# One attention kernel, three double score tiles: two of them take scores and pairs of row maxima by turns

## The chip, the core and the metric

The kernel runs on one core of one Trainium2 chip. It is one launch that computes a whole transformer block in float32 (most matmuls read fp32r operands that were split into a high and a low part, so that three products stand for one exact one). The metric is device time in microseconds. Before the change it is 1136.1 us, the median of three runs between 1134.84 and 1137.12. Five engines work side by side, each in the order of its own queue: TensorE (PE; PEld is its weight load), VectorE (DVE), ScalarE (ACT), GpSimd (POOL) and SyncE (SP), which issues nearly all DMAs. PSUM, into which TensorE writes, has 8 banks of 128 x 512 float32; all of this case turns on who holds which bank for how long.

## The reference, cut to what matters

One sequence of S = 2048 tokens, D = 448, H = 16 heads of 28, a hidden width F = 1792:

```python
h = layernorm(x) * (1 + ca) + sa                 # sa, ca, ga, sb, cb, gb from silu(c) @ w_mod
q, k, v = split(h @ wqkv)                        # 16 heads of 28
p = softmax(q @ k^T * 28 ** -0.5)                # 16 x 2048 x 2048
x = x + ga * ((p @ v) @ wo)
h = layernorm(x) * (1 + cb) + sb
x = x + gb * (gelu(layernorm(h) @ w1 + b1) @ w2 + b2)
```

The softmax needs the maximum of every row of scores before the exponential of that row is taken. The kernel finds these maxima in a pass of its own, from the high parts of q and k alone, and then computes the scores a second time, exactly, with the negated maximum as one more row of the product.

## The kernel before, in words

The program has three stages. In the first one (about 175 us) q, k and v are computed and the first maxima are taken. The second one is the attention: 16 units, each of one group g of four heads and one quarter qt of 512 queries, and in each unit 16 steps of 128 keys, 256 steps in all. The third one is the MLP.

A step of the attention (lines 1142 to 1183 of the kernel before) does this, and the order in which the lines stand is the order of each engine's queue, since the schedule is written out by hand.

- Scores of 128 keys by 512 queries for four heads: each head has a row group of the PE array (32 of its 128 rows). Two halves of two heads (`hf`, rows 0 to 63 and 64 to 127) go each into one double tile of two banks (`ps_s2`, lines 90 to 93), three products per head (`term`): 12 matmuls at line 1163. ScalarE takes the exponential of a whole double tile in one instruction (line 1168) and writes half of the tile of probabilities `pt`.
- Row maxima, three or four of them (`n_maxima`, line 1122): each is a matmul of one head's 128 queries by 512 keys into one single bank (`max_mm`, line 466) and a VectorE reduction of 128 x 512 to one column (`max_one`, line 471). `emit_max` (line 565) takes them from the queue `mxq`; those beside the first half are from heads of the other half, those behind the second half are from heads of the first.
- The product of the probabilities of the step before with v (`av`, line 1133): 4 matmuls in the program, 8 in the trace (float32 takes two), into the bank `o`. The text calls it AV.
- What the schedule `sched` has for the step (line 1182): the end of a unit (division by the row sums, DMAs through DRAM), the projection with `wo` in four steps of each of the last four units (`t_wo`, line 912: 9 or 12 matmuls at line 386 into a single bank, a copy by ScalarE at line 926), preparation of weights.

The maxima of the next unit have to be complete six steps before it begins: `finish_max` (line 610, called at line 1147) takes what is still missing, one after the other.

The 8 banks in this stage before: `o` has one, the maxima have three single banks by turns (`mx_ring`: m1, m2, m2), the scores have two double tiles (`s_ring`: s1, s0). Once all maxima are taken, `third_tile` (line 800) gives the two banks of m2 to a third double tile s2 for the scores. `slot` gives buffers in SBUF by name: `pt` goes round d0, c0 and c1, which hold other things in the first and the third stage.

## Time and profile before

| what | us |
|---|---|
| median of three runs | 1136.1 |
| span of the profiled execution | 1133.1 |
| runs, lowest to highest | 1134.84 to 1137.12 |
| attention, the 232 stretches from AV to AV that have maxima in them (175.15 to 770.95) | 595.8 |
| TensorE busy over the span | 1123.2 |
| VectorE busy over the span | 843.6 |
| ScalarE busy over the span | 671.4 |

The profile is of one execution, whose span is 3.0 us below the median of the runs. Its parts are: busy time by engine; the chain of work that ended last; groups of instructions by line, with their number, busy time, mean duration in ns and the idle time before them; the waits (who waited for whom: total us, times, longest); windows (busy us of PE, PEld, DVE, ACT, POOL in a stretch, with counts, the granted clock as a share of full speed, and the DMA share); and the timeline (start in us, duration in us, engine, line, operation, names, number of instructions merged into the row). A row of the timeline that merges several instructions has the start of the first and the time until the end of the last. Matmuls are pipelined, so TensorE shows as busy nearly all the time even where it waits; where a matmul starts says more than how busy the engine is.

### The profile page before, as it was taken

How to read it: one execution, taken by the hardware profiler on the slowest of the kernel's cores; microseconds unless marked ns; L12 is line 12 of the kernel's file. 1: busy time of each engine (PE TensorE's matmuls, PEld its weight loads, DVE VectorE, ACT ScalarE, POOL GpSimd, SP SyncE). 2: the span in 40 equal slices, each digit the busy share in tenths (PEclk: the TensorE clock that was granted, in tenths of full speed). 3: DMA queues.
4: the chain of work that ended last, by engine and by line, in shares of the span. 5: the costliest groups of instructions: out<-in, count | busy, mean ns of one | idle time of the engine just before them, and what ended most of it. 6: DMA issues, size and time to landing. Idle time of an engine off the chain costs nothing.

```text
span 1133.1 us, 20660 instructions
## 1 busy us (share of the span) xinstructions
PE 1123.2 (99%) x8319; PEld 673.8 (59%) x8319; DVE 843.6 (74%) x1485; ACT 671.4 (59%) x823; POOL 209.8 (19%) x211
## 2 busy tenths in 40 slices
PE   9999999999999999999999999999999999999998
PEld 6756674444444444444444454545468888888887
DVE  6868788999999999999999978595348853444322
ACT  4555667777777877787787867576862321211110
POOL 2533332010000000000000010207114503123000
PEclk9999999999999999999999999999999999999999
DMA  8562263121221211211111312020422100000000
GB/s 309 203 206 77 86 213 100 46 85 39 68 84 57 58 39 57 86 57 58 48 48 57 104 49 76 11 85 1 136 57 86 43 33 1 1 33 1 33 1 33
DMA packets 49341, 81.19 MB, mean 72 GB/s; under 512 B 12311, under 2 KB 18702, under 8 KB 49234
## 3 DMA queue, kind: packets, MB, share of 16 engines
q1 hardware_dynamic: 48762, 79.14, 22.2%
q8 instruction: 65, 1.06, 0.4%
q10 hardware_dynamic: 148, 0.46, 0.1%
q0 software_dynamic: 336, 0.28, 0.1%
q14 instruction: 30, 0.25, 0.1%
HBM read 55.04 MB, written 26.48 MB: 72 GB/s over the span
## 4 chain that ended last, share of the span: by engine, by line
PE 93%; DVE 3%; DMA 1%; ACT 1%; issue 1%; SPq 0%; DVEq 0%; POOL 0%; POOLq 0%; ACTq 0%
PE s L1163 27%; PE o L1133 22%; PE m L386 16%; PE pa L386 8%; PE m L466 6%; PE s L1233 3%; PE s L1232 3%; PE s L1234 3%; DVE mxp L471 2%; PE t L1233 1%; PE t L1234 1%; PE t L1232 1%; PE o L267 1%; PE ma L466 1%; DMA slot_c<-in_w_mod_dram 1%
## 5 line engine op out<-in xcount | busy, mean ns | idle before, releaser
L471 DVE TENSOR_REDUCE mxp<-m 128x1 f32<-128x512 f32 x884 | 568.8, 685 | 81.4 <-PE m L466 44.6
L1163 PE MATMUL s<-slot_b,slot_a 28*128 28x512 f32 (+1 forms) x3072 | 383.3, 422 | 0.3
L1168 ACT ACTIVATE slot_c<-s 128x1024 f32<-128x1024 f32 x340 | 329.6, 1022 | 82.4 <-PE s L1163 82.2
L1163 PEld LDWEIGHTS s<-slot_b,slot_a 28*128 28x128 f32 (+1 forms) x3072 | 216.4, 184 | 251.3 <-ACT slot_c L1168 149.4
L466 PE MATMUL m<-kh,qh 28*128 28x512 f32 x863 | 286.0, 472 | 0.9 <-DVE mxp L471 0.5
L1168 ACT ACTIVATE slot_d<-s 128x1024 f32<-128x1024 f32 x172 | 166.8, 1022 | 42.1 <-PE s L1163 42.0
L1133 PE MATMUL o<-slot_c,v 128*32 128x512 f32 x1360 | 181.2, 605 | 0.0
L1209 ACT ACTIVATE full<-m,b_col 128x512 f32<-128x512 f32 x56 | 38.6, 688 | 191.9 <-PE m L386 179.7
L1212 DVE CAST hi<-full 128x512 fp32r<-128x512 f32 x56 | 25.2, 450 | 135.2 <-ACT full L1209 135.2
L466 PEld LDWEIGHTS m<-kh,qh 28*128 28x128 f32 x863 | 114.3, 182 | 6.6 <-DVE mxp L471 4.7
L895 POOL TENSOR_TENSOR osb<-osb,osb 128x512 f32<-128x512 f32 x16 | 20.9, 1308 | 448.3 <-DMA osb<-drec 306.9
L1133 PE MATMUL o<-slot_d,v 128*32 128x512 f32 x688 | 92.5, 605 | 0.6 <-ACT osb L1102 0.4
L386 PE MATMUL m<-y,slot_a 128*128 128x512 f32 x160 | 60.7, 395 | 0.0
L1133 PEld LDWEIGHTS o<-slot_c,v 128*32 128x32 f32 x1360 | 26.8, 108 | 53.5 <-issue 52.8
L1213 DVE TENSOR_TENSOR lo<-full,hi 128x512 fp32r<-128x512 f32 x56 | 44.1, 788 | 5.9 <-DVE hi L1212 0.9
L386 PE MATMUL m<-y,slot_c 128*128 128x512 f32 x152 | 47.5, 396 | 0.1
L471 DVE TENSOR_REDUCE mxp<-ma 128x1 f32<-128x512 f32 x54 | 35.6, 682 | 7.2 <-PE m L466 4.1
L386 PE MATMUL m<-y,slot_v 128*128 128x512 f32 x112 | 39.2, 396 | 0.0
L386 PE MATMUL m<-y,slot_b 128*128 128x512 f32 x112 | 39.0, 397 | 0.0
L479 ACT ACTIVATE slot_d<-m 128x512 f32<-128x512 f32 x33 | 18.8, 597 | 31.5 <-PE m L466 18.0
L1234 PE MATMUL s<-slot_v,lo 128*128 128x448 f32 x96 | 35.0, 365 | 0.0
L1232 PE MATMUL s<-slot_v,hi 128*128 128x448 f32 x96 | 35.0, 364 | 0.0
(272 smaller groups left out, 1434.0 us busy)
## 6 DMA issues: line engine op xcount, KB each, us to landing
slot_b<-d SPq DMA_DIRECT2D x32, 256.0 KB
slot_a<-d SPq DMA_DIRECT2D x32, 256.0 KB
d<-lo SPq DMA_DIRECT2D x28, 256.0 KB
d<-hi SPq DMA_DIRECT2D x16, 256.0 KB
osb<-drec SPq DMA_DIRECT2D x15, 256.0 KB
out_dram<-xn SPq DMA_DIRECT2D x16, 224.0 KB
raw<-in_B_w_dram SPq DMA_DIRECT2D x14, 224.0 KB
qh<-d SPq DMA_DIRECT2D x12, 256.0 KB
```

The source lines that it names most:

```text
L386: pe.matmul(p, a, b, start=(i == 0), stop=(i == len(terms) - 1))
L466: pe.matmul(m, qh_sb[(g, qt)][js, i * 128 : (i + 1) * 128], k[js, :], start=True, stop=True)
L471: dve.tensor_reduce(out=mxp[(g, qt)][:, i, j, cch : cch + 1], in_=m, op=ALU.max, axis=AX.X)
L1133: pe.matmul(o[32 * j : 32 * j + 32, :], v_sb[kt // 4][:, kt % 4, 4 * g + j, :], p[:, j, :], start=(kt == 0), stop=(kt == NKT - 1),)
L1163: pe.matmul(s2[:, jj, :], ks[rows_, kp, kc], qs[rows_, qp, :], start=(term == 0), stop=(term == 2))
L1168: act.activation(pt[:, 2 * hf : 2 * hf + 2, :], s2, AF.Exp, scale=SCALE)
L1209: act.activation(gf, p, AF.Gelu_apprx_tanh, bias=b1_col[:, i : i + 1])
L1212: dve.tensor_copy(ghi, gf)
L1213: dve.tensor_tensor(out=glo, in0=gf, in1=f(ghi), op=ALU.subtract)
L1232: pe.matmul(pp, ghi[:, ts], w_hi, start=(m == 0), stop=False)
L1233: pe.matmul(pp, ghi[:, ts], w_lo, start=False, stop=False)
L1234: pe.matmul(pp, glo[:, ts], w_hi, start=False, stop=(m == NFT - 1))
```

## The change

The 8 banks of the attention stage are dealt out anew. `o` and m1 keep one bank each; s0, s1 and s2 are three double tiles from the start.

- The first half of a step's scores always goes to s0. The second half goes to s1 or s2 by turns (`now`), and the other one of these two takes a pair of maxima: two matmuls of two heads of one half, and one VectorE reduction of 128 x 2 x 512 to two columns (`emit_pair`). Single maxima have the one bank m1 (`emit_single`).
- Which half of the heads comes first changes from step to step, so that the pair behind the second half is of heads of the first one, and the single one beside the first half of heads of the second one.
- A plain step has one single maximum and one pair. In some steps (`extra`) a second single stands between the pair and AV; there the first single stands behind the third product of the first half, and in the step after such a one behind the first product of the second half.
- A step with a `wo` projection issues first a pair of maxima into s0, then a single one into one bank of the tile `now`, and the projection into its other bank: three maxima more than a plain step.
- The probabilities of a step are two tiles of half the size; those of the first half have three buffers, those of the second two. The names c0, c1 and d0 in SBUF are halved for that, also where the first and third stage use them.

The order of the built program, engine by engine, shows what comes of it in the 232 stretches from AV to AV that have maxima in them. Before: 223 plain ones, 114 with three maxima and 109 with four in turn, and nine with a projection (three or four maxima, the last one two). After: 66 plain ones with a second single, most of them every third step, 155 with three maxima, two in which `finish_max` adds 6 and 4 maxima, one after the other through m1, and nine with a projection, mostly with six maxima, two of which have 6 and 4 more from `finish_max`. The reductions of VectorE fall from 946 to 706, 240 of them pairs. No DMA is added or removed in the attention.

```diff
-    halved = ("a2", "a3", "b1")
+    halved = ("a2", "a3", "b1", "c0", "c1", "d0")
...
+    def ps_two(key):
+        return ps_pools[key][1].tile([128, 2, 512], F32, tag=key, name=nm(key), bufs=1)
...
-    def emit_max(n, half=None):
+    def emit_max(n):
...
+    def ready_max():
+        return [m for m in mxq[:24] if (m[0], m[2]) in kh_sb and m[:2] in qh_sb]
...
+    def emit_single(half, ps):
...
+        near = ready_max()
...
+        fits = [x for x, m in enumerate(near) if m[4] // 2 == half]
+        alone = [x for x in fits if whole[by_set(near[x])] == 1]
+        m = near[alone[0] if alone else fits[-2] if len(fits) > 1 else 0]
...
+        max_one(g, qt, cch, i, j, ps)
+        count(g, qt, [cch])
+
+    def emit_pair(half, t):
+        near = ready_max()
+        for a, m in enumerate(near):
+            n = m[:4] + (m[4] + 1,)
+            if m[4] == 2 * half and n in near:
...
+                for jj in range(2):
+                    max_mm(g, qt, i, j + jj, kh_sb[(g, cch)], lambda: t[:, jj])
+                dve.tensor_reduce(out=mxp[(g, qt)][:, i, j : j + 2, cch], in_=t, op=ALU.max, axis=AX.X)
+                count(g, qt, [cch, cch])
+                return
+        for jj in range(2):
+            emit_single(half, lambda: t[:, jj])
...
-    for key in ("ma", "pa"):
+    for key in ("ma", "pa", "m2"):
         ps_close(key)
     for key in ("s0", "s1"):
         ps_open(key)
-    s_ring[:] = ["s1", "s0"]
-    mx_ring[:] = ["m1", "m2", "m2"]
...
+    ps_open("s2", "right")
+    mx_ring[:] = ["m1"]
+    turns = ("s1", "s2")
...
         def t_wo(t):
             def go():
-                p = ps_mx()
+                if three:
+                    p = ps_mx()
+                else:
+                    emit_pair(0, ps_two("s0"))
+                    two = ps_two(now[0])
+                    emit_single(1, lambda: two[:, 1])
+                    p = two[:, 0]
...
+    def extra(s_):
         n_plain, n_wo = left_steps(s_)
-        over = len(mxq) - 7 * n_plain // 2
...
+        over = len(mxq) - 3 * n_plain - 6 * n_wo
+        if is_wo(s_) or n_plain == 0:
+            return False
+        due[0] += max(over, 0) / n_plain
+        if due[0] < 1:
+            return False
+        due[0] -= 1
+        return True
...
-    ptags = ["d0", "c0", "c1"]
-    done_max = set()
+    ptags = (["d0", "c0", "c1"], ["c0h", "c1h"])
+    after = False
...
-            pt = slot(ptags[step % 3], [128, 4, 512], F32)
-            n = n_maxima(step)
-            n0 = 1 if n == 3 and step % 4 == 3 else 2
-
+            now[0] = turns[step % 2]
+            pt = [slot(tags[step % len(tags)], [128, 2, 512], F32) for tags in ptags]
+            more = not three and extra(step)
+            late_one, after = after, more
             ks, qs = kst[(g, kt // 4)], qst[u]
             kc = slice((kt % 4) * 128, (kt % 4 + 1) * 128)
-            for hf in range(2):
-                s2 = ps_s2()
+            for n, hf in enumerate((step % 2, 1 - step % 2)):
+                s2 = ps_s2() if three else ps_two((now[0] if n else "s0"))
                 for term, (kp, qp) in enumerate(((0, 0), (1, 0), (0, 1))):
                     for jj in range(2):
...
-                    if hf == 0 and term < min(n0, n):
-                        emit_max(1, 1)
-                    if hf == 1 and term == 2 and n > n0:
-                        emit_max(n - n0, 0)
-                act.activation(pt[:, 2 * hf : 2 * hf + 2, :], s2, AF.Exp, scale=SCALE)
+                    if (n, term) == ((0, 2) if more else (1, 0) if late_one else (0, 0)):
+                        emit_single(1 - step % 2, ps_mx)
+                    if n == 1 and term == 2 and mxq:
+                        emit_pair(step % 2, ps_two(turns[1 - step % 2]))
+                    if n == 1 and term == 2 and more:
+                        emit_single(step % 2, ps_mx)
+                act.activation(pt[hf], s2, AF.Exp, scale=SCALE)
...
-    third_tile(False)
+    ps_close("s2")
+    ps_open("m2", "right")
+    s_ring[:] = ["s1", "s0"]
+    mx_ring[:] = ["m1", "m2", "m2"]
```

More of the change, by code (lines that the diff above doesn't have):

```diff
@@ L78, in slot, with slot4 @@
         return sb.tile(shape, dt, tag="slot_" + tag, name=nm("slot_" + tag), bufs=1)
-    halved = ("a2", "a3", "b1")
-    def slot4(tag, inner):
+    halved = ("a2", "a3", "b1", "c0", "c1", "d0")
+    def slot4(tag, inner, dt=F32R):
         if tag not in halved:
-            t = slot(tag, [128, 4] + inner)
+            t = slot(tag, [128, 4] + inner, dt)
             return lambda k: t[:, k]
-        t2 = [slot(tag + h, [128, 2] + inner) for h in ("", "h")]
+        t2 = [slot(tag + h, [128, 2] + inner, dt) for h in ("", "h")]
         return lambda k: t2[k // 2][:, k % 2]
+    def ps_two(key):
+        return ps_pools[key][1].tile([128, 2, 512], F32, tag=key, name=nm(key), bufs=1)
     def ps_s2():
         s_ring.append(s_ring.pop(0))
-        key = s_ring[-1]
-        return ps_pools[key][1].tile([128, 2, 512], F32, tag=key, name=nm(key), bufs=1)
+        return ps_two(s_ring[-1])
     def ps_s():
@@ L121, in tile_adaln_block @@
     sa_col, ca_col = cols[:, 0:NC], cols[:, NC:]
-    d0 = slot("d0", [128, 4, 512], F32)
-    sil_b = d0[:, 0, 0 : NC * 32].rearrange("p (k r) -> p k r", r=32)
-    c_rows = d0[0:NC, 1, :128]
+    d0 = slot4("d0", [512], F32)
+    sil_b = d0(0)[:, 0 : NC * 32].rearrange("p (k r) -> p k r", r=32)
+    c_rows = d0(1)[0:NC, :128]
     sp.dma_start(c_rows[0:3], c[0, 0:384].rearrange("(k p) -> k p", p=128))
@@ L162, in mod_part @@
         return slice(64 * h, 64 * h + 64), slice(j * D, (j + 1) * D)
-    wm_ac = [slot(f"c{i}", [128, 2, 2 * D], F32) for i in range(2)]
+    wm_ac = [slot(f"c{i}{h}", [128, 2 * D], F32) for i in range(2) for h in ("", "h")]
     for k in range(NC):
-        load_mod(wm_ac[k // 2][:, k % 2, :], k, 0, 2)
+        load_mod(wm_ac[k], k, 0, 2)
     load_w(slice(0, 2 * D), lambda k: raw_qk[k // 2][:, k % 2, :])
@@ L311, in tile_adaln_block @@
             pe.matmul(
-                pm[32 * j : 32 * j + 32, :D], sil_b[rs_, k, :], wm_ac[k // 2][rs_, k % 2, cs],
+                pm[32 * j : 32 * j + 32, :D], sil_b[rs_, k, :], wm_ac[k][rs_, cs],
                 start=(k == 0), stop=(k == NC - 1),
@@ L351, in by_head @@
         return t.rearrange("(j r) n -> j r n", r=32)
-    ones = d0[0:4, 0, 128:384]
+    ones = d0(0)[0:4, 128:384]
     pool.memset(ones, 1.0)
@@ L476, in pair_diff @@
         m = max_mm(g, qt, i, j, k_diff[0])
-        r = d0[:, 1 + px_no[0] % 3]
+        r = d0(1 + px_no[0] % 3)
         px_no[0] += 1
@@ L560, in count @@
                     load_hi(0, g + 1, qt)
-    last_j = [None]
-    def emit_max(n, half=None):
+    def emit_max(n):
         for _ in range(n):
@@ L568, in emit_max, with by_set @@
                 return
-            fits = [x for x, m in enumerate(mxq[:32]) if half is None or (m[4] // 2 == half and m[4] != last_j[0])]
-            g, qt, cch, i, j = mxq.pop(fits[0] if fits else 0)
-            last_j[0] = j
+            g, qt, cch, i, j = mxq.pop(0)
             max_one(g, qt, cch, i, j)
             count(g, qt, [cch])
+    def ready_max():
+        return [m for m in mxq[:24] if (m[0], m[2]) in kh_sb and m[:2] in qh_sb]
+    def by_set(m):
+        return (m[:4], m[4] // 2)
+    def emit_single(half, ps):
+        if not mxq:
+            return
+        near = ready_max()
+        whole = {}
+        for m in near:
+            whole[by_set(m)] = whole.get(by_set(m), 0) + 1
+        fits = [x for x, m in enumerate(near) if m[4] // 2 == half]
+        alone = [x for x in fits if whole[by_set(near[x])] == 1]
+        m = near[alone[0] if alone else fits[-2] if len(fits) > 1 else 0]
+        mxq.remove(m)
+        g, qt, cch, i, j = m
+        max_one(g, qt, cch, i, j, ps)
[5 more added lines that the diff above has]
+            if m[4] == 2 * half and n in near:
+                mxq.remove(m)
+                mxq.remove(n)
+                g, qt, cch, i, j = m
+                for jj in range(2):
+                    max_mm(g, qt, i, j + jj, kh_sb[(g, cch)], lambda: t[:, jj])
+                dve.tensor_reduce(out=mxp[(g, qt)][:, i, j : j + 2, cch], in_=t, op=ALU.max, axis=AX.X)
+                count(g, qt, [cch, cch])
+                return
+        for jj in range(2):
+            emit_single(half, lambda: t[:, jj])
     def emit_task(n, sixth, n_pairs):
@@ L796, in tile_adaln_block @@
         ps_open(key)
-    s_ring[:] = ["s1", "s0"]
-    mx_ring[:] = ["m1", "m2", "m2"]
-    def third_tile(on):
-        ps_close("m2" if on else "s2")
-        ps_open("s2" if on else "m2", "right")
-        s_ring[:] = s_ring + ["s2"] if on else ["s1", "s0"]
-        mx_ring[:] = ["m1"] if on else ["m1", "m2", "m2"]
+    ps_open("s2", "right")
+    mx_ring[:] = ["m1"]
+    turns = ("s1", "s2")
     phase1[0] = False
@@ L1023, in go @@
                 else:
-                    t = slot(tags[0], [128, 2, NC, 256])
-                    w1t[q] = [lambda k: t[:, 0, k], lambda k: t[:, 1, k]]
+                    w1t[q] = [lambda k, t=slot(tag, [128, NC, 256]): t[:, k] for tag in tags]
             hi, lo = w1t[q][0](k), w1t[q][1](k)
@@ L1092, in tile_adaln_block @@
     items += [w2_item(ft, ("d0", q1)) for ft in range(8, 12)]
-    items += [w1_item(3, k, ("c1",)) for k in range(NC)]
+    items += [w1_item(3, k, ("c1", "c1h")) for k in range(NC)]
     items += [w2_item(ft, ("e0",)) for ft in range(12, NFT)]
@@ L1108, in tile_adaln_block @@
     o = None
-    plain = [0]
+    due = [0.0]
+    now = [None]
     three = False
@@ L1119, in left_steps @@
         return len(rest) - n_wo, n_wo
-    def n_maxima(s_):
+    def extra(s_):
         n_plain, n_wo = left_steps(s_)
-        over = len(mxq) - 7 * n_plain // 2
-        if is_wo(s_):
-            return max(0, -(-over // max(n_wo, 1)))
-        plain[0] += 1
-        return 4 if plain[0] % 2 or (over > 3 * n_wo and over > 0) else 3
+        over = len(mxq) - 3 * n_plain - 6 * n_wo
[6 more added lines that the diff above has]
+        return True
     def av(u, kt, p, o):
@@ L1133, in av @@
             pe.matmul(
-                o[32 * j : 32 * j + 32, :], v_sb[kt // 4][:, kt % 4, 4 * g + j, :], p[:, j, :],
+                o[32 * j : 32 * j + 32, :], v_sb[kt // 4][:, kt % 4, 4 * g + j, :], p[j // 2][:, j % 2, :],
                 start=(kt == 0), stop=(kt == NKT - 1),
             )
-    ptags = ["d0", "c0", "c1"]
-    done_max = set()
+    ptags = (["d0", "c0", "c1"], ["c0h", "c1h"])
+    after = False
     for u in range(NU):
@@ L1150, in tile_adaln_block @@
                 three = True
-                third_tile(True)
-            pt = slot(ptags[step % 3], [128, 4, 512], F32)
-            n = n_maxima(step)
-            n0 = 1 if n == 3 and step % 4 == 3 else 2
+                s_ring[:] = ["s0", turns[step % 2], turns[1 - step % 2]]
+            now[0] = turns[step % 2]
+            pt = [slot(tags[step % len(tags)], [128, 2, 512], F32) for tags in ptags]
+            more = not three and extra(step)
+            late_one, after = after, more
             ks, qs = kst[(g, kt // 4)], qst[u]
             kc = slice((kt % 4) * 128, (kt % 4 + 1) * 128)
-            for hf in range(2):
-                s2 = ps_s2()
+            for n, hf in enumerate((step % 2, 1 - step % 2)):
+                s2 = ps_s2() if three else ps_two((now[0] if n else "s0"))
                 for term, (kp, qp) in enumerate(((0, 0), (1, 0), (0, 1))):
@@ L1163, in tile_adaln_block @@
                         pe.matmul(s2[:, jj, :], ks[rows_, kp, kc], qs[rows_, qp, :], start=(term == 0), stop=(term == 2))
-                    if hf == 0 and term < min(n0, n):
-                        emit_max(1, 1)
-                    if hf == 1 and term == 2 and n > n0:
-                        emit_max(n - n0, 0)
-                act.activation(pt[:, 2 * hf : 2 * hf + 2, :], s2, AF.Exp, scale=SCALE)
+                    if (n, term) == ((0, 2) if more else (1, 0) if late_one else (0, 0)):
[5 more added lines that the diff above has]
+                act.activation(pt[hf], s2, AF.Exp, scale=SCALE)
             if step == 0:
                 v_task(NB - 1, 3, ps_mx())
-                emit_max(2)
             if pend is not None:
```

## The prediction, made before the result was known

> **What bounds the kernel now.** I read the page first, then windows of the attention, the waits there, and the timeline of single steps.

> ```profile
> span 1133.1 us, 20660 instructions
> PE 1123.2 (99%) x8319; PEld 673.8 (59%) x8319; DVE 843.6 (74%) x1485; ACT 671.4 (59%) x823; POOL 209.8 (19%) x211
> L471 DVE TENSOR_REDUCE mxp<-m 128x1 f32<-128x512 f32 x884 | 568.8, 685 | 81.4 <-PE m L466 44.6
> ```

> TensorE is busy 99% of the span, but its rows overlap, so that says little; VectorE waits 44.6 us for maxima in all (the last row). The part the change touches is the stretch from the first AV to the last maxima, 595.80 us (a window: busy us of TensorE, its weight loads, VectorE at 531.74 or 89%, ScalarE, GpSimd; the granted clock is 1.00):

> ```profile
> 175.15:770.95 595.80, 594.74 (x5544) 273.54 (x5543) 531.74 (x878) 461.26 (x487) 60.11 (x64) 1.00 0.20 60
> ```

> ```profile
> PEld s L1163 <- ACT slot_c L1168: 149.4, 222, 1.1
> ...
> PEld s L1163 <- ACT slot_d L1168: 74.2, 111, 0.9
> ```

> In that window the weight loads of the scores wait 149.4 + 74.2 = 223.6 us for exponentials, five times what VectorE waits for its work. So the scores' tiles set the pace, not the reductions. Two steps show it, first with three maxima (from 505.78), then with four (from 507.97), TensorE and then ScalarE:

> ```profile
> 505.78 0.50 PE L1163 MATMUL s<-slot_b,slot_a 29*128 29x512 f32 x2
> ...
> 506.57 0.41 PE L466 MATMUL m<-kh,qh 28*128 28x512 f32 x2
> 506.65 0.40 PE L1163 MATMUL s<-slot_b,slot_a 28*128 28x512 f32 x2
> 506.97 1.06 PE L1133 MATMUL o<-slot_c,v 128*32 128x512 f32 x8
> 507.97 0.50 PE L1163 MATMUL s<-slot_b,slot_a 29*128 29x512 f32 x2
> 507.98 0.51 PE L466 MATMUL m<-kh,qh 28*128 28x512 f32 x2
> 508.30 1.02 PE L1163 MATMUL s<-slot_b,slot_a 28*128 28x512 f32 x6
> ...
> 509.17 0.40 PE L1163 MATMUL s<-slot_b,slot_a 28*128 28x512 f32 x2
> 509.29 0.49 PE L466 MATMUL m<-kh,qh 28*128 28x512 f32 x1
> 509.39 0.40 PE L1163 MATMUL s<-slot_b,slot_a 28*128 28x512 f32 x2
> 509.73 1.06 PE L1133 MATMUL o<-slot_d,v 128*32 128x512 f32 x8
> 510.72 0.49 PE L1163 MATMUL s<-slot_b,slot_a 29*128 29x512 f32 x2
> ```

> ```profile
> 506.84 1.94 ACT L1168 ACTIVATE slot_d<-s 128x1024 f32<-128x1024 f32 x2 [0.81 <-PE s L1163]
> 509.03 1.94 ACT L1168 ACTIVATE slot_c<-s 128x1024 f32<-128x1024 f32 x2 [0.26 <-PE s L1163]
> ```

> In the first step both halves run side by side and AV follows 1.19 after the first score; in the second, the second half waits for the exponential that ends at 506.84 + 1.94 = 508.78, starts at 508.83 (the row below), and AV is 1.76 behind. The lengths are 2.19 and 2.75, mean 2.47.

> ```profile
> 508.83 0.18 PEld L1163 LDWEIGHTS s<-slot_b,slot_a 29*128 29x128 f32 x2 [0.33 <-ACT slot_d L1168]
> ```

> **Prices.** From these rows: the second product starts .33 behind the first (507.97, 508.30), each further one .22 (509.17, 509.39); AV .33 behind the last product (509.39, 509.73); the next scores 1.00 behind AV (506.97, 507.97); the first exponential 1.06 behind the first score (507.97, 509.03); the second .92 behind the first (two take 1.94, one 1.02); .05 from its end to the waiting matmul. A matmul right after a wait loads its weights first (.49 instead of .40), so AV is .43 behind it (509.29, 509.73). For single maxima and reductions:

> ```profile
> 508.54 0.69 DVE L471 TENSOR_REDUCE mxp<-m 128x1 f32<-128x512 f32 x1
> ```

> ```profile
> 711.19 0.22 DVE L502 TENSOR_REDUCE m<-mxp 128x16 fp32r<-128x64 f32 x1
> ...
> 713.50 1.88 DVE L471 TENSOR_REDUCE mxp<-m 128x1 f32<-128x512 f32 x3
> ```

> ```profile
> 714.24 0.50 PE L466 MATMUL m<-kh,qh 28*128 28x512 f32 x1 [0.21 <-DVE mxp L471]
> ```

> A maximum's reduction starts .56 behind its matmul (507.98, 508.54) and lasts .69; queued ones follow each other by .60 (three in 1.88); its bank takes the next matmul .05 after its end (713.50 + .69, 714.24). One bank alone thus serves a maximum each .56 + .69 + .05 = 1.30. No row has a reduction of 1024. From 64 to 512 elements it grows from .22 to .685, 1.04 ns each, so 512 more cost .53: the pair takes 1.22, an estimate between 1.07 (two times that slope alone) and 1.37 (two singles). I take 1.22, since the slope is of the same instruction.

> [...]

> **The change, part by part** (times from the first score of a step).

> *Plain step, one single and one pair (N).* s0 is taken again when its exponential is read: 1.06 + 1.02 + .05 = 2.13, a floor. The pair's tile was read by the second exponential of the step before: 1.06 + .92 + 1.02 + .05 = 3.05 after that step's first score, 3.05 − P in this one. AV queues behind the pair, .43 later, the next step 1.00 after that: P = 4.48 − P, P = 2.24. Three maxima in 2.24, where the old pair of steps has seven in 4.94: 0.75 against 0.71 each.

> *Step with a second single (M).* The first single sits behind the third product, but its row group is idle and weights go one product ahead, so it starts at .34; reduction .90 to 1.59; m1 free at 1.64. The second single waits for that, and AV stands behind it on TensorE: AV at 2.07, step 3.07. Nothing covers it: the exponentials are done by 3.0 and wait for the next scores.

> *The step after (L).* Its single stands in the second half, on one of that half's row groups, which then has four passes (load .10, then .44, .66, .88, 1.11): AV at 1.44, step 2.44. Its reduction starts at 1.12, so the pair's (matmuls at 1.00) starts at 1.72 and ends at 2.94. *The next (N after L):* its second half goes to that tile, free at 2.99, which is .55: passes at .66, .89, 1.12, AV at 1.45, step 2.45.

> Three such steps take 3.07 + 2.44 + 2.45 = 7.96 for ten maxima. The same prices give the old four-maxima step: second half at .86, last product at 1.42, AV 1.75, 2.75, as its row has.

> *Projection steps.*

> ```profile
> 669.30 0.88 PE L386 MATMUL m<-slot_e,slot_a2h 128*128 128x448 f32 x3
> ...
> 671.33 0.50 PE L1163 MATMUL s<-slot_b,slot_a 29*128 29x512 f32 x2
> ```

> ```profile
> 715.96 1.07 PE L1133 MATMUL o<-slot_c,v 128*32 128x512 f32 x8
> 716.96 0.86 PE L386 MATMUL m<-slot_e,slot_a2h 128*128 128x448 f32 x3
> ...
> 719.59 0.50 PE L1163 MATMUL s<-slot_b,slot_a 29*128 29x512 f32 x2
> ...
> 720.74 0.64 PE L1133 MATMUL o<-slot_d,v 128*32 128x512 f32 x4
> ```

> Nine matmuls take 2.03 (669.30 to 671.33), twelve 2.63 (716.96 to 719.59); a step with twelve was 4.78 long (715.96 to 720.74). Now the single maximum and the projection share the tile that the second exponential has just been given: AV ends at 2.24 and that exponential at 3.05, so TensorE idles some .5 (the pair in s0 fits in); the single starts at 3.05, the projection .43 later at 3.48, the next score at 5.51 or 6.11. Four and five of them: 52.6, for three maxima more each.

> *What `finish_max` adds:* 20 maxima through m1 alone, at the head of a step where nothing else can run: 20 × 1.30 = 26.0; before there were three banks and no such row of singles. From below, .60 each (12), if ring and queue hid the rest; I take 1.30, since one bank leaves no other order.

> *At nothing:* the smaller tiles of probabilities (AV of two steps before is issued ahead of the scores that would wait), the halved names in the first and third stage, the three double tiles after the last maximum (the old program had them there too). Cover gone, each is within 1 us.

> **Sum.** 66 × 7.96 = 525.4; 23 N left × 2.24 = 51.5; the two steps that `finish_max` precedes 3.07 + 2.44 = 5.5; 52.6; 26.0: 661.0 instead of 595.8, +65.2. Span 1198.3; the median stands 3.0 above the span: 1201.

> Bounds: the pair's reduction, −7 to +12. The wait of the second single: the cheapest extra maximum in the rows is the fourth of the old steps, 2.75 − 2.19 = .56 instead of M's .83 and no after-effects: 3 × 2.24 + .56 = 7.28, −45. The singles of `finish_max`, −14.

> **Rivals.**
> *Extras at the old price.* The queue of VectorE and the next steps absorb the second single: 1201 − 45 = 1156. For it: the old fourth maximum had its waits too. Against: m1 is the only single bank, and AV stands behind it.
> *Faster: VectorE sets the pace.* 240 pairs save .15 each (1.37 − 1.22), 36 us; if the stage is as long as its reductions, 1100. For it: 531.7 of 595.8 busy. Against: it waits for TensorE, and a queued reduction starts each .60, so seven need 4.2 of 4.94. It decides only if the extra waits of TensorE all fit into VectorE's time. [...]
> *Slower still: strict order on TensorE.* If no matmul may start ahead of an earlier one of another row group, M's first single starts at .55 (+.21), the second half too: L +.11, N +.09; 66 × .32 + 2 = 23 more, 1224. Against: at 506.57 maxima issued behind the second half start ahead of its last product at 506.65. [...]
> *No change:* the steps' gain and loss cancel; that needs −65, nearly all bounds at once.

> **How the numbers follow.** 1201: chance .66, its own range 1180 to 1222. Extras at the old price .18, 1140 to 1178. Faster .07, strict order .06, no change (within .2%, about what a measurement here tells apart) .03. I leave out the faster one, no change, and what lies above 1222: 1150 to 1222. Faster .07, same .03, slower .90.

> **What would show it.** AV to AV of 3.07, 2.44, 2.45 by turns; a row of waits of TensorE for single reductions of some 40 us and more; reductions of 128x1024 near 1.22; projection steps near 6.1; four or six singles 1.3 apart at four places. It is wrong if the steps with a second single are under 2.8, or if the second half does not wait for the pair's reduction.

## The result, and the profile after

The changed kernel takes 1260.2 us, the median of runs between 1254.9 and 1264.0, against 1136.1 before: a ratio of 1.109, 95% interval 1.107 to 1.112. It is slower, as forecast, but by 124 us where 65 were forecast, and 1260 lies well outside the range of 1150 to 1222.

The profiled execution has a span of 1258.1 us, 125.0 more than before. The page of the changed kernel (span; busy time by engine; the clock in 40 slices of 31 us; the two groups of reductions):

```profile
span 1258.1 us, 20550 instructions
PE 1183.1 (94%) x8319; PEld 696.3 (55%) x8319; DVE 822.4 (65%) x1245; ACT 672.1 (53%) x823; POOL 209.5 (17%) x211
PEclk9999997979999999999999886879899999999999
L473 DVE TENSOR_REDUCE mxp<-m 128x1 f32<-128x512 f32 x390 | 265.6, 686 | 178.7 <-PE s L1202 94.2
L604 DVE TENSOR_REDUCE mxp<-s 128x2 f32<-128x1024 f32 x240 | 293.0, 1221 | 41.7 <-PE s L1202 36.3
```

The pair's reduction takes 1.221 us, as estimated, and VectorE has less to do than before (822 us instead of 844). But it idles 178.7 us ahead of single reductions. And the clock row is not all nines: it falls to between 6 and 8 in the slices near 200 and 265 us and in six slices between 690 and 910 us.

Windows of the changed kernel, first the same 232 stretches from AV to AV (busy us of TensorE, its loads, VectorE, ScalarE, GpSimd; granted clock; DMA share; GB/s), then three parts of them:

```profile
176.12:893.80 717.68, 656.91 (x5550) 297.27 (x5551) 513.03 (x642) 462.08 (x487) 60.74 (x65) 0.94 0.16 50
300.00:400.00 100.00, 95.38 (x868) 41.67 (x872) 78.00 (x99) 73.32 (x78) 7.84 (x9) 1.00 0.21 65
200.00:300.00 100.00, 88.68 (x702) 37.92 (x698) 66.90 (x88) 58.96 (x63) 6.94 (x8) 0.86 0.14 41
735.00:780.00 45.00, 34.06 (x167) 18.96 (x165) 21.80 (x28) 11.43 (x14) 4.76 (x5) 0.70 0.00 1
```

So 121.9 of the 125.0 us are in these stretches (717.7 instead of 595.8), and the granted clock over them is 0.94 where it was 1.00. Over the whole span the mean clock is 0.963; as the trace's records of the clock hold only full and half, that is 1258.1 x 0.037 x 2 = 93 us at half clock.

The waits of the changed kernel in that window (who waited for whom: total us, times, longest):

```profile
DVE mxp L473 <- PE s L1202: 94.2, 135, 2.8
...
PEld m L468 <- DVE mxp L473: 78.9, 90, 1.5
...
PEld s L1202 <- ACT slot_c1h L1209: 65.0, 77, 1.1
...
PEld s L1202 <- ACT slot_c L1209: 61.6, 71, 1.7
```

New are the first row, VectorE waiting for the end of a score product although what it reduces is a maximum, and the size of the second, TensorE waiting for the bank of a single maximum (3.0 us in the same stretches before).

Sorted by kind of step, the 717.7 us stand against the 661.0 forecast like this (sums of the lengths from AV to AV in the trace; the forecast's 13.0 for ten singles is put with the steps in which they fall):

| steps | forecast | measured | difference |
|---|---|---|---|
| 221 plain steps | 576.9 | 602.6 | +25.7 |
| 2 plain steps with 6 and 4 singles from `finish_max` | 18.5 | 20.1 | +1.6 |
| 9 projection steps, two of them with 6 and 4 singles | 65.6 | 94.9 | +29.3 |

Of the 25.7 us in the first row, 17.4 are what eleven steps take above the usual length of their kind (3.21 with four maxima; with three 2.66, the longest of the three usual lengths): the first one, those behind rows of singles (3.2 us) or beside projections (3.6), and four near 270 (9.1). The other 210 plain steps were priced nearly right; 48 of the 57 us that were missing lie in 22 steps.

**Regular steps.** TensorE of the changed kernel from 671.14, then VectorE:

```profile
671.14 0.62 PE L1172 MATMUL o<-slot_c,v 128*32 128x512 f32 x2
...
672.13 0.50 PE L1202 MATMUL s<-slot_b,slot_a 29*128 29x512 f32 x2
...
673.79 0.62 PE L1172 MATMUL o<-slot_d,v 128*32 128x512 f32 x2
...
674.79 0.49 PE L1202 MATMUL s<-slot_b,slot_a 29*128 29x512 f32 x2
674.81 0.50 PE L468 MATMUL m<-kh,qh 28*128 28x512 f32 x1
675.12 0.84 PE L1202 MATMUL s<-slot_b,slot_a 28*128 28x512 f32 x8
...
676.57 0.49 PE L468 MATMUL m<-kh,qh 28*128 28x512 f32 x1 [0.37 <-DVE mxp L473]
676.99 0.62 PE L1172 MATMUL o<-slot_c,v 128*32 128x512 f32 x2
...
677.98 0.81 PE L1202 MATMUL s<-slot_b,slot_a 29*128 29x512 f32 x7
678.34 0.44 PE L468 MATMUL m<-kh,qh 28*128 28x512 f32 x1
...
679.18 0.62 PE L1172 MATMUL o<-slot_c,v 128*32 128x512 f32 x2
```

```profile
675.82 0.69 DVE L473 TENSOR_REDUCE mxp<-m 128x1 f32<-128x512 f32 x1 [0.64 <-PE s L1202]
676.43 1.22 DVE L604 TENSOR_REDUCE mxp<-s 128x2 f32<-128x1024 f32 x1
```

From AV to AV: 2.65 (N), 3.20 (M), 2.19 (L). In M the first maximum starts right beside the first score (674.81), though it stands behind the third product in the queue; but its reduction starts 1.01 behind it (675.82), not .56. It waits, as the row says, for a score product. The second single then follows the old sum: 675.82 + .69 + .06 = 676.57, and AV .42 later.

**Singles of `finish_max`.** TensorE from 200.16:

```profile
200.16 0.49 PE L468 MATMUL m<-kh,qh 28*128 28x512 f32 x1
201.52 0.49 PE L468 MATMUL m<-kh,qh 28*128 28x512 f32 x1 [0.87 <-DVE mxp L473]
202.79 0.50 PE L468 MATMUL m<-kh,qh 28*128 28x512 f32 x1 [0.78 <-DVE mxp L473]
204.07 0.79 PE L468 MATMUL m<-kh,qh 28*128 28x512 f32 x1 [0.78 <-DVE mxp L473]
205.65 0.79 PE L468 MATMUL m<-kh,qh 28*128 28x512 f32 x1 [0.78 <-DVE mxp L473]
207.22 0.79 PE L468 MATMUL m<-kh,qh 28*128 28x512 f32 x1 [0.78 <-DVE mxp L473]
...
211.09 1.07 PE L1172 MATMUL o<-slot_d,v 128*32 128x512 f32 x2
...
214.97 1.07 PE L1172 MATMUL o<-slot_c,v 128*32 128x512 f32 x2
```

At first they are 1.27 to 1.36 apart, near the forecast (1.30). But from the fourth on a matmul takes .79 instead of .49, the spacing grows to 1.58, and AV, 3.9 us behind the last of the six, still runs at half pace (1.07 instead of .62). The two steps behind take 3.88 and 3.15.

**Projection steps.** TensorE, then VectorE, in the first of the nine:

```profile
738.47 0.62 PE L1172 MATMUL o<-slot_c,v 128*32 128x512 f32 x2
...
740.19 0.49 PE L468 MATMUL s<-kh,qh 28*128 28x512 f32 x1 [0.22 <-ACT slot_c0h L1209]
741.96 0.88 PE L388 MATMUL s<-slot_e,slot_a2h 128*128 128x448 f32 x3 [1.28 <-DVE mxp L473]
```

```profile
740.08 1.23 DVE L604 TENSOR_REDUCE mxp<-s 128x2 f32<-128x1024 f32 x1 [0.22 <-PE s L468]
741.22 0.68 DVE L473 TENSOR_REDUCE mxp<-s 128x1 f32<-128x512 f32 x1
```

The single is where the forecast had it. The projection does not follow .43 behind it: it waits until the single's reduction, which queues behind the pair's, has ended at 741.90. The two write different banks of one double tile.

**A stall that the forecast did not have.** TensorE near 270:

```profile
267.56 0.49 PE L468 MATMUL s<-kh,qh 28*128 28x512 f32 x1 [0.78 <-DVE mxp L473]
...
276.38 0.76 PE L468 MATMUL m<-kh,qh 28*128 28x512 f32 x1 [3.29 <-DMA kh<-d]
```

No pair is at hand here, so `emit_pair` puts two singles into one double tile, and the second waits for the first one's reduction. In the next step, 9.08 long, a maximum of a later group of keys is taken whose load has not landed.

### The profile page after: what moved, and what is told of

The parts are those of the page before. It is cut to its first block, busy times and chain, and to the rows that moved or that the text cites. A ratio compares the mean times of both kernels' runs of the same rounds, so it can differ in the third digit from the quotient of the medians.

```text
span 1258.1 us, 20550 instructions
## 1 busy us (share of the span) xinstructions
PE 1183.1 (94%) x8319; PEld 696.3 (55%) x8319; DVE 822.4 (65%) x1245; ACT 672.1 (53%) x823; POOL 209.5 (17%) x211
## 3 DMA queue, kind: packets, MB, share of 16 engines
q8 instruction: 65, 1.06, 0.4%
## 4 chain that ended last, share of the span: by engine, by line
PE 86%; DVE 9%; DMA 2%; issue 1%; ACT 1%; POOL 0%; SPq 0%; DVEq 0%; ACTq 0%; POOLq 0%
PE s L1202 23%; PE o L1172 20%; PE m L388 12%; PE pa L388 8%; DVE mxp L473 7%; PE m L468 5%; PE s L388 3%; PE s L1276 3%; PE s L1277 3%; PE s L1275 3%; PE s L468 2%; DVE mxp L604 1%; PE t L1276 1%; PE t L1277 1%; PE t L1275 1%
## 5 line engine op out<-in xcount | busy, mean ns | idle before, releaser
L473 DVE TENSOR_REDUCE mxp<-m 128x1 f32<-128x512 f32 x390 | 265.6, 686 | 178.7 <-PE s L1202 94.2
L604 DVE TENSOR_REDUCE mxp<-s 128x2 f32<-128x1024 f32 x240 | 293.0, 1221 | 41.7 <-PE s L1202 36.3
L1209 ACT ACTIVATE slot_c<-s 128x1024 f32<-128x1024 f32 x170 | 173.5, 1022 | 83.0 <-PE s L1202 81.6
L468 PE MATMUL m<-kh,qh 28*128 28x512 f32 x369 | 175.2, 500 | 44.6 <-DVE mxp L473 39.9
L1209 ACT ACTIVATE slot_c1h<-s 128x1024 f32<-128x1024 f32 x128 | 131.2, 1025 | 83.8 <-PE s L1202 78.7
L1172 PE MATMUL o<-slot_c1h,v 128*32 128x512 f32 x512 | 140.0, 626 | 0.0
L1172 PE MATMUL o<-slot_c0h,v 128*32 128x512 f32 x512 | 137.5, 616 | 0.0
L1209 ACT ACTIVATE slot_c0h<-s 128x1024 f32<-128x1024 f32 x128 | 130.5, 1019 | 4.1 <-PE s L1202 2.3
L468 PE MATMUL s<-kh,qh 28*128 28x512 f32 x494 | 111.2, 439 | 4.0 <-DVE mxp L473 2.1
L1209 ACT ACTIVATE slot_d<-s 128x1024 f32<-128x1024 f32 x86 | 87.8, 1021 | 36.1 <-PE s L1202 35.9
L1172 PE MATMUL o<-slot_d,v 128*32 128x512 f32 x344 | 94.2, 627 | 1.5 <-ACT slot_d L1209 1.1
```

The lines of the kernel that those rows point to most:

```text
L468: pe.matmul(m, qh_sb[(g, qt)][js, i * 128 : (i + 1) * 128], k[js, :], start=True, stop=True)
L473: dve.tensor_reduce(out=mxp[(g, qt)][:, i, j, cch : cch + 1], in_=m, op=ALU.max, axis=AX.X)
L604: dve.tensor_reduce(out=mxp[(g, qt)][:, i, j : j + 2, cch], in_=t, op=ALU.max, axis=AX.X)
L1172: pe.matmul(o[32 * j : 32 * j + 32, :], v_sb[kt // 4][:, kt % 4, 4 * g + j, :], p[j // 2][:, j % 2, :], start=(kt == 0), stop=(kt == NKT - 1),
L1209: act.activation(pt[hf], s2, AF.Exp, scale=SCALE)
```

## The experiments

My theory after reading this: the missing 57 us come from places where TensorE has little to do. There it waits, and there its clock is halved, for longer than the place lasts (near 200 it is .50 from 203.5 to 217.2, and the last of the six singles ends at 208.0). The rival: the denser plain steps cost more than I priced, everywhere. Times are medians (of two runs each but for the first row, which has four), ratios are to runs of the kernel before on the same chip (1135.0 to 1135.4 there); the mean clock and the "stage", the sum of the 232 stretches, are of the profiled run.

| kernel | us | ratio (95%) | mean clock | stage |
|---|---|---|---|---|
| after | 1260.2 | 1.109 (1.107, 1.112) | .963 | 717.6 |
| before + singles (e8) | 1170.8 | 1.031 (1.028, 1.035) | .987 | 629.9 |
| fill, 28 rows (e2) | 1268.1 | 1.117 (1.113, 1.120) | .963 | 725.7 |
| fill, 64 rows (e13) | 1277.6 | 1.125 (1.120, 1.131) | .961 | 730.8 |
| fill, 128 rows (e7) | 1253.4 | 1.104 (1.091, 1.117) | .977 | 715.1 |
| projection's single in m1 (e3) | 1232.5 | 1.085 (1.076, 1.095) | .979 | 686.2 |
| second singles by due date (e5) | 1239.8 | 1.092 (1.088, 1.097) | .972 | 695.5 |
| second single behind AV (e4) | 1252.0 | 1.103 (1.099, 1.106) | .963 | 708.2 |
| first single at once (e6) | 1235.0 | 1.088 (1.084, 1.091) | .965 | 692.5 |
| pair one product earlier (e9) | 1259.0 | 1.109 (1.106, 1.112) | .963 | 716.0 |
| e3 + e5 + no double single (e11) | 1207.1 | 1.064 (1.061, 1.067) | .994 | 661.6 |
| e11 + e6 (e12) | 1189.3 | 1.048 (1.045, 1.051) | .991 | 642.3 |
| e12 + e9 (e10) | 1174.4 | 1.035 (1.032, 1.038) | .996 | 628.8 |

**The singles alone, put into the kernel before (e8).** Twenty additional singles through m1, which compute nothing that is used, at the four places where the changed kernel has its own.

```diff
                 finish_max(*divmod(u + 1, NB))
+                for g_, qt_, cch_, i_, j_ in mxq[: {0: 6, 11: 4, 12: 6, 13: 4}.get(u, 0)]:
+                    m_ = ps_tile("m1")
...
+                    pe.matmul(
+                        m_, qh_sb[(g_, qt_)][js, i_ * 128 : (i_ + 1) * 128], kh_sb[(g_, cch_)][js, :],
...
+                    dve.tensor_reduce(out=scr, in_=m_, op=ALU.max, axis=AX.X)
```

> The kernel before, with 6, 4, 6 and 4 more single maxima, one after the other through m1, at the steps where the changed kernel has its 20 (their results go to a column nobody reads): the disputed cost by itself. Theory A (waiting, and the halved clock behind it): 20 x 1.27 = 25 for the chain, 8 to 14 more for matmuls at half clock, 1168 to 1176. Rival B (waiting alone, as predicted): 1159 to 1163.

1170.8: the first theory. TensorE of this kernel:

```profile
199.96 0.50 PE L1152 MATMUL m<-kh,qh 28*128 28x512 f32 x1 [0.78 <-DVE scr L1156]
201.24 0.79 PE L1152 MATMUL m<-kh,qh 28*128 28x512 f32 x1 [0.78 <-DVE scr L1156]
...
206.38 1.94 PE L1133 MATMUL o<-slot_d,v 128*32 128x512 f32 x8
```

The stage is 34 us longer (629.9 instead of 595.8) for 20 singles; 20 x 1.28 are 25.6, and the rest lies in steps that the trace has at half clock (.79 for a matmul, 1.94 for AV instead of 1.06). The tiles, the pairs and the order of the change have no part in it: the row of singles does it by itself.

**What keeps the clock up (e2, e13, e7).** Useless matmuls behind each single of `finish_max` fill the time in which TensorE waits for the bank: five of 28 rows, four of 64, or four of 128.

```diff
         while left[(g, qt)] > 0:
+            m = mxq[0]
             emit_max(1)
+            if not phase1[0]:
+                t = ps_two("s0")
+                for _ in range(4):
+                    pe.matmul(t[:, 0, :], qh_sb[m[:2]][:, 0:128], kh_sb[(m[0], m[2])], start=True, stop=True)
```

> The changed kernel (1260.2 us), with five matmuls of 0.22 us into s0, whose result nobody reads, behind each of the 20 single maxima that finish_max adds: TensorE no longer idles there, the chain of singles stays 1.27 each. Theory A (the halved clock is brought on by TensorE's idle time, here in the chain of singles): the granted clock stays at 1 behind the first such place, the two steps after it fall from 3.89 and 3.15 to about 2.3; 10 to 16 us less in all, 1244 to 1250. Rival B (the singles cost their waiting alone, and the clock has another cause): within 3 us of 1260, and the same places at half clock.

> As the kernel with five matmuls behind each single of finish_max, which kept one row group of 32 rows busy and left the clock at half at the same places (1268.1 us): now four matmuls over all 128 rows, 0.22 each, in their place. Theory A (the clock goes by how much of the array works, so that one row group in four does not hold it): the clock stays at 1 behind the four places, the two steps after each take 2.2 to 2.4 instead of 3.9; 10 to 16 us less than the changed kernel, 1244 to 1250. Rival B (the clock falls for a reason that no filling touches): the places stay at half clock, 1258 to 1270.

> As e7_fill_full, but the four matmuls behind each single of finish_max use 64 of the 128 rows. Theory A (the clock follows the share of the array that works, and half of the rows all the time is enough, as in the plain steps, where pairs of 32-row matmuls run side by side): full clock at 198 and 693, mean .977 and about 1253 like e7_fill_full. Theory B (it takes more than half): half clock at 198 and 693 as in the changed kernel, mean .963, 1262 to 1268.

The window from 200 to 210 us in the changed kernel, then with 28, 64 and 128 rows (TensorE's busy time first, the granted clock behind GpSimd's):

```profile
200.00:210.00 10.00, 6.00 (x24) 2.95 (x21) 5.52 (x9) 1.99 (x3) 0.91 (x1) 0.68 0.07 17
```

```profile
200.00:210.00 10.00, 9.88 (x32) 6.18 (x31) 3.80 (x7) 0.00 (x0) 0.00 (x0) 0.72 0.00 0
```

```profile
200.00:210.00 10.00, 10.00 (x23) 5.27 (x21) 3.08 (x5) 0.00 (x0) 0.00 (x0) 0.61 0.00 0
```

```profile
200.00:210.00 10.00, 9.86 (x44) 5.37 (x42) 4.51 (x8) 0.32 (x2) 0.03 (x1) 1.00 0.02 5
```

TensorE is busy 9.9 to 10 of 10 us in all three, and the clock is 0.72, 0.61 and 1.00. So being busy isn't enough: with matmuls of 28 or 64 rows, one at a time, the clock fell within the row of singles; with those of 128 rows it stayed full here, and in the rows near 690 (1.00 from 690 to 700) and 750 as well. At the fourth place it did not. There the clock had fallen at 818.2, in the projection ahead, and it stayed at half through the whole row, though TensorE was busy all the time, with the same singles and matmuls of 128 rows:

```profile
820.20:831.20 11.00, 11.00 (x21) 5.78 (x20) 2.98 (x5) 0.53 (x1) 1.19 (x2) 0.50 0.00 0
```

So the number of rows makes a difference, but it is not the whole rule. The expectation for 28 rows was missed, and so was the first one for 64; that for 128 rows held at three of four places, and the time lies between its two forecasts. With 128 rows the two steps behind the singles near 200 and 690 have their usual length again. In time e7 gains little, 7 us with an interval that reaches from 8 above the changed kernel's median to 22 below it: the filling itself costs (its spacing is 1.55), and the two runs had different clocks (.977 at 1259.6, .987 at 1247.2).

**The projection's single in m1 (e3).**

```diff
-                    emit_single(1, lambda: two[:, 1])
+                    emit_single(1, ps_mx)
```

> The changed kernel, with the single maximum of a projection step in m1 instead of beside the projection in one tile. Theory A (the projection waits for that single's reduction, since both are in one tile): it starts some 0.4 instead of 1.5 behind the single, 9 x 1.1 = 10 us less, and up to 15 more where TensorE's clock no longer halves there: 1235 to 1250. Rival B (it is the second exponential that holds the tile, as the prediction had it): within 3 us of 1260.

```profile
821.12 0.49 PE L468 MATMUL m<-kh,qh 28*128 28x512 f32 x1
822.01 0.88 PE L388 MATMUL s<-slot_e,slot_a2h 128*128 128x448 f32 x3 [0.40 <-ACT slot_d L1209]
```

1232.5, 28 us less for one word, a little more than expected. TensorE now waits for the exponential that last read the tile, as the prediction had it, and not for VectorE; six of the nine projection steps take 4.9 to 6.1, and all nine 66.4 instead of 94.9, where the forecast had 65.6. Most of the half clock in them goes too (17 us instead of 53); what is left is at the two steps with rows of singles and just behind them.

**Singles spread by due date (e5).** Beside the even spread, a step is given a second single when the next unit's maxima would otherwise be late, and close to that date singles are taken from that unit first; 84 steps have a second single, and `finish_max` finds 3 maxima missing instead of 20.

```diff
+        first, end = (u_ + 1, NKT - 6) if kt_ < NKT - 6 else (u_ + 2, 2 * NKT - 6)
...
+            room = sum(6 if is_wo(s_ + x) else 3 for x in range(end - kt_))
+            if sum(m[:2] == divmod(first, NB) for m in mxq) > room - 4:
...
+                return True
```

> No rows of singles: the second singles are placed by the date at which a unit's maxima are due, so that finish_max has 3 maxima left instead of 20 and 84 steps have a second single instead of 66; all else as in the changed kernel. Theory A (the 20 singles cost their 1.30 each, and after them some 13 us of half clock): the two rows ahead of plain steps (11.92 and 8.18) and the two ahead of projections give back 27 us and some 10 of half clock, and 17 more second singles cost 1.07 each (8.06 for the triple instead of 3 x 2.33), 18: 1236 to 1246, granted clock above .970, full clock at 198 and 693. Theory B (the singles only pay where others would have to be paid: a maximum costs about the same in any place): within 6 of 1260.

1239.8, as the first theory had it; the rows of singles are gone. One part was missed: its first steps all have a second single now, the first AV is 5 us later, and four steps of 5 us each run at half clock, which gives back much of it. The placement alone does not do that. e11 below has the same order of work up to 200 us on VectorE and ScalarE, and full clock there. The same window, first e5, then e11:

```profile
176.00:198.00 22.00, 20.86 (x101) 8.51 (x99) 9.78 (x12) 9.31 (x10) 3.12 (x4) 0.50 0.18 47
```

```profile
176.00:198.00 22.00, 19.93 (x160) 9.34 (x157) 15.99 (x21) 13.80 (x15) 4.33 (x6) 1.00 0.18 49
```

Why the clock fell in the one and not in the other, no run shows; the times below can hold some us of such luck.

**The second single behind AV (e4)**, so that AV does not wait for m1.

```diff
-                    if n == 1 and term == 2 and more:
-                        emit_single(step % 2, ps_mx)
...
+            if more:
+                emit_single(step % 2, ps_mx)
             if kt == 0:
```

> The changed kernel, with the second single of a step issued behind AV instead of ahead of it. Theory A (AV is held up by that single's wait for m1, as the prediction had it): such a step falls from 3.21 to about 2.5, the one after rises to some 2.65; three steps take 7.8 instead of 8.06, 15 to 20 us less in all, 1240 to 1246. Rival B (the wait only moves: what VectorE has to do sets the three steps): within 5 us of 1260.

1252.0: between the two. M's wait is .83 in each of 66 steps by the forecast, 55 us; the stage gets 9 us shorter. So the wait mostly moves into the next step, whose scores now stand behind the second single.

**The first single at once (e6).** The first single of a step with two stands behind the first product, not the third.

```diff
-                    if (n, term) == ((0, 2) if more else (1, 0) if late_one else (0, 0)):
+                    if (n, term) == ((1, 0) if late_one and not more else (0, 0)):
```

> The changed kernel, with the first single of a step that has two issued behind the first product of the first half, as in a plain step, instead of behind the third. Theory A (a matmul that starts early still reports in the order of the queue, so that the single's reduction waits for the third product's end): its reduction starts at about 0.6 instead of 1.03, the second single and AV come 0.45 earlier, such a step takes 2.75 instead of 3.21: 66 x 0.45 = 30 us less, 1230. Rival B (the single's own wait for m1 or VectorE sets its reduction): the step keeps 3.2, within 5 us of 1260.

```profile
640.76 0.50 PE L1202 MATMUL s<-slot_b,slot_a 29*128 29x512 f32 x2
640.77 0.50 PE L468 MATMUL m<-kh,qh 28*128 28x512 f32 x1
```

```profile
641.34 0.69 DVE L473 TENSOR_REDUCE mxp<-m 128x1 f32<-128x512 f32 x1
```

1235.0, 25 us less. The maximum starts where it did before, .01 behind the first score. But its reduction now starts .57 behind it and not 1.01, and M falls from 3.21 to 2.74. L gives some of it back (2.51 instead of 2.19) and the N behind it gains (2.41 instead of 2.66); three steps take 7.66 instead of 8.06. So this matmul starts ahead of earlier ones in the queue (674.81 and 675.12 in the changed kernel), but VectorE begins on its result only behind their end: 1.01 behind the start where the third product stands ahead of it, .57 where only the first does. Of the 94.2 us in which VectorE waited for scores with a single reduction, 11.3 are left.

**The pair one product earlier (e9).**

```diff
-                    if n == 1 and term == 2 and mxq:
+                    if n == 1 and term == 1 and mxq:
```

> The changed kernel, with the pair of maxima issued ahead of the second half's third product instead of behind it. Theory A (the pair reports in the order of the queue, so its reduction waits for the third product; that reduction then holds up the next second half): the reduction starts 0.2 earlier, plain steps with three maxima fall from 2.33 to 2.2, three steps from 8.06 to some 7.8: 15 to 20 us less, 1240 to 1245. Rival B (the pair's tile, read by the second exponential of the step before, then holds up the third product as well): no less, 1255 to 1270.

1259.0: no gain by itself. In M the pair's reduction follows the single's without a gap (676.43 above), so it is the single's that comes late.

**Together (e11, e12, e10).** e11 has the edits of e3 and e5, and emits one single where no pair is at hand; e12 has e6's as well, e10 e9's on top.

```diff
-        for jj in range(2):
-            emit_single(half, lambda: t[:, jj])
+        emit_single(half, lambda: t[:, 0])
```

> Three places at once where TensorE had little to do: the date-wise placement of e5_due, the projection's single in m1 (e3_wo_own), and a single maximum where no pair is at hand, instead of two in one double tile. The order of the plain steps is untouched (first single behind the third product, pair behind the last). Theory A (the rest is what denser plain steps cost at full clock): e3_wo_own gives 28, the placement some 19, the fallback some 8: 1200 to 1210; granted clock .990 and more; triples still 3.2, 2.2, 2.65. Theory B (stalls and half clock spill over into plain steps far from them): below 1190.

> As e11_no_idle, and the first single of a step with two stands behind the first product instead of the third (e6_first). Theory A: 84 such steps are .3 to .47 shorter each, 25 to 35 less than e11_no_idle, 1168 to 1178 (the variant with all five edits had 1174, the early pair among them, which alone brought nothing). It stays above before's 1136 since 84 steps of 2.8 and 138 of 2.3 take more than before's 109 of 2.75 and 114 of 2.19 for their maxima. Theory B (the early pair is worth something once the other waits are gone): 1182 or more.

> The changed kernel with its found costs taken away together: first single ahead in steps with two, the single of a projection step in m1, the pair ahead of the third product, one maximum instead of two in one tile where no pair is at hand, and second singles put where a unit's maxima would come late, so that finish_max adds 3 instead of 20. If these are the causes: the clock stays at 1 nearly throughout, 232 stretches of some 223 x 2.25 + 84 x 0.6 + 9 x 5.4 = 601, about 1140 to 1160. If something else is left: over 1175.

e11 came out as expected, 1207.1: without the idle places the stage is 56 us shorter than the changed kernel's 717.6, and nearly all of the half clock goes with them (mean .994). Its M steps stay at 3.21, so the rival (stalls spill far into the plain steps) falls. e12 missed the first forecast, 1168 to 1178, and came out as the other had it: 1189.3. The rest is in e10, 15 us lower, whose only other edit is the early pair. VectorE in the same step with a second single, first e12, then e10:

```profile
457.35 1.23 DVE L613 TENSOR_REDUCE mxp<-s 128x2 f32<-128x1024 f32 x1 [0.23 <-PE s L1219]
```

```profile
448.57 1.23 DVE L613 TENSOR_REDUCE mxp<-s 128x2 f32<-128x1024 f32 x1
```

Once the single's reduction is early, VectorE waits .23 for the last scores (the first row) before it begins on the pair, which stands behind them; put one product ahead, the pair is ready when the single is reduced, and the second row has no wait. The step behind such a one falls from 2.52 to 2.27; the N after that rises from 2.41 to 2.57; a step with a second single right behind another such one falls from 3.16 to 3.01. So an edit that brought nothing alone brings something here, but not all of the 15 us: e12 has half clock from 171.8 to 188.9 and e10 for 3.4 us there, and its first AV is 1.6 later and its first two steps 2.0 longer than later ones of their kind.

e10 missed as well (1140 to 1160 was expected): it is still 3.5% slower than before, and its first AV is 4 us later. Its stage is 33 us longer than before. By the two traces 9.5 of that are projection steps (51.3 instead of 41.7). Some 7 are what four steps between 251 and 274 take above the usual length of their kind; in two of them a load of keys is still awaited (1.53 and 1.86 us), a wait that no variant of the changed kernel is without. The rest, about 17, is in the regular steps: a step with a second single takes 2.74, and 3.01 where it follows another such one (28 of 84); those with three maxima 2.2 to 2.6, where before it was 2.75 and 2.19. A kernel without the twenty maxima was not tried.

## Why the prediction was right and wrong

The sum came out 57 us short. The steps of it that failed are "the projection .43 later" and `finish_max` without what follows it; missing from it was the wait for a pair and for a load near 270.

- *Direction and plain steps: right.* The three steps of a triple were forecast at 7.96 and measured 3.21 + 2.19 + 2.66 = 8.06, a lone N 2.33 instead of 2.24; the pair 1.221 instead of 1.22. M waits for m1 with AV behind it, as the sum said.
- *L and the N after it: the place of the wait was wrong, its sum right.* The single in L's second half did not cost a fourth pass (2.19, not 2.44). The pair's reduction ends when forecast, so the next second half waits longer instead (2.66, not 2.45). The load that waits, in the N at 672.13:

```profile
672.89 0.18 PEld L1202 LDWEIGHTS s<-slot_b,slot_a 29*128 29x128 f32 x2 [0.23 <-DVE mxp L604]
```

  .76 behind the first score, where I had .55.
- *M, "reduction .90 to 1.59": mis-sized.* It starts 1.03 behind the first score. I had the matmul's start wrong in the other direction (.34; it is .02), and took its end for the moment VectorE may begin. The rival of strict order was half right: starts are not in order (674.81 before 675.12), but what VectorE waits for goes by the order of the queue (1.01 behind the start here, .57 in e6).
- *Projection steps, 52.6: the step that failed is "the projection .43 later".* I treated the two banks of `two` as free of each other. The tile is guarded as one: the projection waits for the single's reduction and starts 3.49 behind AV (738.47 to 741.96) instead of 2.24 (3.48 less the 1.24 of AV). That is 1.25 in each of nine steps, 11 us, and the one such step that is wholly at full clock is 1.14 above its forecast (7.25 instead of 6.11). The other 18 of the 29 us lie in steps with half clock, 53 of their 95 us; e3 brought the kernel 28 back.
- *`finish_max`, 26.0: the singles are right (1.27 apart), their consequence was missing.* I read the granted clock of 1.00 in the profile before as a property of the stage. It was one of the work in it: e8 halves it in the kernel before (a matmul takes .79 there instead of .50, and the mean clock is .987). In the changed kernel the four plain steps behind the two rows of singles cost 3.2 us more than usual; the other two rows stand in projection steps, and what half clock adds there is in the 29 us above.
- *Not in the sum at all:* `emit_pair` without a pair, and the load of keys that comes late; the four steps near 270 are 9 of the 17.4 us.
- *The range* took its upper end from the pair's reduction and from strict order, that is from plain steps; no bound took in a stretch where TensorE has nothing to do, and that is where most of the missing time went. (By the terms shown the pair's lower bound is 66 x .15 = 10, not 7; nothing hangs on it.) Of the rivals, the old price for extras (1156) fell with M at 3.21; e6 shows that one line would have brought M to 2.74, its price, but three steps only to 7.66, where the rival had 7.28.

## What to carry to other kernels

A granted clock of 1.00 in a profile is no promise for another order of work (e8), and e5 and e11 had different clocks on the same one (.50 and 1.00 from 176 to 198); where a change leaves TensorE with nothing but a chain of single matmuls that wait for another engine, price the half clock behind it too (in the changed kernel the clock fell 3.4 us behind the first single at 200.16, and 4.8 behind that at 693.64). Here two users of one double tile waited for each other though they used different banks; a bank of its own for one of them brought 28 us. Put a matmul whose reader is urgent early in the queue itself: here starting early was not enough, since the reader went by the order of the queue (its reduction came 1.01 behind the start, and .57 in e6).
